# The shift of the exponentials, formed by two subtractions on GpSimd from the fifth pair on, and a new order of all work

## The chip, the cores and the metric

The kernel runs on one core of one Trainium2 chip. Its time is device microseconds of one execution, from the host's side of the launch to the end; a profiled execution also has a span, from the first to the last instruction on the engines. The engines are TensorE (PE in the profile), VectorE (DVE), ScalarE (ACT), GpSimd (POOL) and SyncE (SP, which only issues DMAs here).

## The reference

Eight batches of eight heads of random-feature attention over 576 positions with head size 64 and 128 features, and behind it one dense layer pair (SiLU between) over all 4608 rows, everything in float32:

```python
def phi(x):
    proj = np.einsum('bhsd,md->bhsm', x, omega)
    sq = np.sum(x * x, axis=-1, keepdims=True) / 2.0
    h = proj - sq
    h = h - np.max(h, axis=-1, keepdims=True)
    return np.exp(h) / np.sqrt(m)
kv = np.einsum('bhsm,bhsd->bhmd', k_p, v)
z = np.sum(k_p, axis=2)
num = np.einsum('bhsm,bhmd->bhsd', q_p, kv)
den = np.einsum('bhsm,bhm->bhs', q_p, z)[..., None] + 1e-06
# attention output num / den, as rows of 512 columns, then
h = x @ w_in                                  # 512 -> 2048
g = h * (1.0 / (1.0 + np.exp(-h)))
return g @ w_out                              # 2048 -> 512
```

The exponent of `phi` is `proj - sq - max(proj - sq)`. As `sq` is the same for a whole row, the kernel takes `m`, the largest `proj` of the row, and forms the shift `nb` that is added to `proj` before the exponential from `m` and `s = sq` (kept as `-(m - s) - s`, rounding as the reference rounds).

## The kernel before

**Attention by pairs of heads.** Two heads make a pair: 32 pairs, `n` from 0 to 31. The 2 x 576 positions of a pair lie in nine chunks of 128 rows, four of one head (chunks 0 to 3), four of the other (5 to 8) and a mixed one (4, "the middle"). For keys (`k`) and then queries (`q`) a pair does this:

- ACT squares the rows (L375) and DVE sums the squares to `sq` (L379);
- PE projects the eight side chunks into two PSUM banks (`project`, L402) and the middle into a third (`project_mid`, L409);
- DVE takes the row maxima `mx` (`top`, L418 for the sides, L416 for the middle);
- `shift` forms `nb`, 128 x 8 for the sides and 128 x 1 for the middle, with two instructions each time (L422, L423). For the first `LEAD` = 4 pairs one call covers all nine chunks;
- then either ACT takes nine exponentials straight from PSUM with `nb` as bias (`expo`, L438, for "straight" pairs), or DVE adds `nb` and writes to SBUF (`lower`, L446 and L443) and ACT takes one exponential over all nine chunks later (`expo_all`, L452). Pairs 0 to 7 and the last ones are straight, the bounds being `DIRECT`, `STRAIGHT_K` and `STRAIGHT_Q`.

The banks of the projection are free for the next matmul only when the exponentials or the lowering have read them. Behind the exponentials come the sums of the keys (`sums` on POOL, L459 to L467, or matmuls, L477 and L479, for the first eight pairs), `kv` (L500), the denominators on DVE (`denom`, L488, ten products, and the reciprocal, L493), the scaling of the queries on POOL (`normal`, L518, three instructions), their transposes on PE (`turn`, L524), and the numerators (L562).

**The dense layers.** The first three row tiles go through plain matmuls (`stage1` L737, `stage2` L983), the other six in three groups of two by a Strassen-like scheme of seven block products (`product` L822, `second` L936). Every operand is held as a high and a low part, so that each product takes three matmuls. The weights are rebuilt from 64-bit words by DVE (L660, L662, L666) and split by POOL (L679, L683) in the first 200 us; later POOL forms the sums of weight blocks that the block products need (L715 to L779), and DVE forms the low parts and block sums of the activations (L880, L869, L902, L926).

**What sets the order.** The whole program is a list of units (`Plan.add`) with an engine, an assumed duration, a due time (`key`), what it waits for and which buffers it takes and frees. `Plan.run` goes through them once, when the kernel is built, and picks for each engine the ready unit that is due first; the instructions of every engine are issued in that order and run in it. Constants (`PRO`, `STAY`, `SPREAD_*`, `PREPARE_*`, `PAIRS_*` and so on) set the due times, and `SHIFTS` lists seeds that move some of them at random. Where a bank is free but PE would idle for over 1.0 us in the first 100 us, the plan puts in matmuls of ones (`pulses`, L351) whose result nobody reads.

A unit of the shift is planned like this (sides; the middle alike):

```python
add(("nb", n, who, 0), "DVE", 0.55, at(n, 0, o + 1.4), lambda n=n, who=who: shift(n, who, sides),
    after=[("top", n, who, j) for j in range(2)] + [("ssum",) + w], port=True)
```

Of the kernel before, what the change touches and what calls it, by code (L numbers as in the profile page):

```python
# [14 lines left out]
ALU = mybir.AluOpType  # L15
# [19 lines left out]

LAG = 2
DIRECT = 8
STRAIGHT_K = 22.298
STRAIGHT_Q = 24.404
NARROW = 4  # L40
AHEAD_OUT = 3
LEAD = 4
# [12 lines left out]
for _f in range(16):  # L55
# [15 lines left out]
START_MLP = 57.593  # L71
SLOW = 8.332
MLP_STEP = 2.725
PRO = 18.178
SWITCH = 1.3
STAY = 19.856
HANDOFF = {"PE": 0.25, "ACT": 0.1, "DVE": 0.1, "POOL": 0.15, "SP": 0.2}
CALM = 0.5
SHIFTS = (
# [3 lines left out]
)  # L83
HOT = 100.0
PULSE = 0.24
# [4 lines left out]


STRETCH_0 = 1.362
SLACK = 0.818
PAIRS_4 = 195.050
PAIRS_16 = 39.198
PAIRS_22 = 540.000
PAIRS_28 = -59.566
SPREAD_IN = 2.859
SPREAD_OUT = 10.456
SPREAD_AT = 366.656  # L100
SPREAD_LATE = 469.554
EARLY_SUMS = 18.806
PREPARE_1 = 22.764
PREPARE_2 = 2.035
LEAD_W = 14.593
PREPARE = (PREPARE_1, PREPARE_2)
BEGIN = [clock(NF * PLAIN)]
BEGIN.append(BEGIN[0] + 56 * MLP_STEP * STRETCH_0)
BEGIN.append(BEGIN[1] + 56 * MLP_STEP * SLACK)
RATE = (STRETCH_0, SLACK, SLACK)  # L110
PACE = ((0, clock(0)), (4, PAIRS_4), (16, clock(NF * PLAIN) - PAIRS_16), (22, PAIRS_22), (28, BEGIN[1] - PAIRS_28))

# [52 lines left out]
class Plan:  # L165
# [6 lines left out]
    def add(self, name, eng, dur, key, fn, after=(), order=(), alloc=(), free=(), banks=0, table=None, lat=0.0, port=False, of="att", reads=()):  # L172
        u = dict(
            name=name, eng=eng, dur=dur, key=key, fn=fn, after=list(after), order=list(order), alloc=list(alloc),
            banks=banks, of=of, table=table, lat=lat, port=port or eng == "POOL", reads=list(reads),
        )
        assert name not in self.units, name
        self.units[name] = u
        for i in free:
            self.freed_by.setdefault(i, []).append(name)  # L180

    def run(self, until=None, heat=None):
# [47 lines left out]
        while any(ready.values()):  # L230
            best = None
            for e, us in ready.items():
                pick, least = None, None
                for u in us:
# [26 lines left out]
                    if u["table"] and u["table"] != table:  # L261
                        key += STAY
                    least = t if least is None else min(least, t)
# [53 lines left out]
def attention_mlp(ctx: ExitStack, tc: tile.TileContext, qT, kT, qn, kn, v, om_in, w_in, w_out, out, out_t):  # L317
    nc = tc.nc
# [100 lines left out]

    def shift(n, who, part):  # L420
        m, s, nb = (part(T[a, n, who]) for a in ("mx", "sq", "nb"))
        nc.vector.tensor_tensor(nb, m, s, ALU.subtract)  # L422
        nc.vector.scalar_tensor_tensor(nb, nb, -1.0, s, ALU.mult, ALU.subtract)  # L423

    def every(a):
        return a[:, :NC]
# [569 lines left out]
    add = plan.add  # L996

    def at(n, off, steady):
        if n < LEAD:
            return PRO * n + off  # L1000
        return pace(n - LEAD - 1 + steady / 32)
# [8 lines left out]
    def straight(n, who):  # L1010
        return n < DIRECT or n >= {"k": STRAIGHT_K, "q": STRAIGHT_Q}[who]

# [3 lines left out]
    for n in range(NWIN):  # L1016
        calm = n < LEAD
        for i, who in enumerate("kq"):
# [20 lines left out]
            o = 6.2 + 10.8 * i  # L1039
# [16 lines left out]
            else:  # L1056
                add(md, "PE", 2.2 if whole else 0.25, at(n, 3 * i + 0.1, o + 5.2),
                    lambda ps, n=n, who=who, f=mid_and_squares if whole else project_mid: f(n, who, ps),
# [7 lines left out]
            if calm:  # L1066
                add(("nb", n, who, 0), "DVE", 0.45, at(n, 3 * i + 1.5, 0), lambda n=n, who=who: shift(n, who, every),
                    after=[("top", n, who, j) for j in range(3)] + ([] if whole else [("ssum",) + w]),
                    free=[bk(md)] if whole else [("ss",) + w], port=True)
            else:  # L1070
                add(("nb", n, who, 0), "DVE", 0.55, at(n, 0, o + 1.4), lambda n=n, who=who: shift(n, who, sides),
                    after=[("top", n, who, j) for j in range(2)] + [("ssum",) + w], port=True)
                add(("nb", n, who, 2), "DVE", 0.45, at(n, 0, o + 5.8), lambda n=n, who=who: shift(n, who, middle),
                    after=[("top", n, who, 2), ("ssum",) + w], free=[("ss",) + w], port=True)
            for j in range(3):
                b = bk(md) if j == 2 else bk(pj, j)
                nb = ("nb", n, who, 0 if calm else j & 2)
# [188 lines left out]
    def second_stage(p):  # L1266
        t1 = lambda i, s: last_time(p, TURNS[p].index(i), s)
        last_of = lambda i: TURNS[p][TURNS[p].index(i) - 1]
        for s in range(NS):
            early = product_time(p, s, 6) + 5 if p else last_time(0, 1, s) - EARLY_SUMS  # L1270
            W = lambda i, s=s: ("ws", p, s, i)
# [3 lines left out]
            for what, after, key in (  # L1275
                ("T3", [W(2), W(3)], early), ("T1", [W(0), G("T3")], early + 1), ("T2", [G("T1"), H(0), L(0)], t1(1, s) - (6 if p else EARLY_SUMS)),
                ("T4", [G("T2"), H(2), L(2), W(1)], last_time(p, 5 if p else 3, s) - (12 if p else 0)),
# [80 lines left out]
    for s in range(NS):  # L1358
        before = ("sp", s - 1, len(sums_of) - 1) if s else ("wlo", "out", NF - 1)
        base = clock(NF + 2 + SPREAD_IN * s)  # L1360
        for i, what in enumerate(sums_of):
# [25 lines left out]
    for s in range(NS):  # L1387
        late = s >= NS // 2
        base = (SPREAD_LATE - SPREAD_OUT * (NS // 2) if late else SPREAD_AT) + SPREAD_OUT * s
        before = [("spo", s - 1, len(out_steps) - 1)] if s else []  # L1390
# [199 lines left out]
```

## Time and profile before

| | |
|---|---|
| median of 2 runs | 1021.25 us (1021.1 to 1021.39) |
| the profiled execution's own time | 1022.64 us |
| its span | 1020.8 us |
| mean granted TensorE clock | 0.990 |
| PE busy | 987.1 us, 97% of the span |
| DVE / ACT / POOL busy | 786.1 / 615.5 / 359.3 us |
| DMA | 232.94 MB, mean 228 GB/s |

PE's busy time counts overlapping matmuls as one stretch, and their ends are modelled; so PE's idle time in a stage is what its busy time leaves of it, and a busy PE can still run at a lowered clock, which the profile lists as the granted clock of a stretch (1.00 is full). The rest of a stage's loss is the busy time multiplied by what the clock lacks. By stage, in us: up to 200 the weights are rebuilt beside the first attention pairs; up to 475 the plain tiles run with one pair every 20 us or so between them; up to 730 the block products of the first group run beside the last pairs; after that only block products are left.

### The profile page before, as it was taken

To read this page: it belongs to the slowest core of one execution; us is meant where nothing else is said; L and a number is where in the kernel's file an instruction comes from. 1 tells how busy PE (TensorE), PEld (TensorE's weight loads), DVE (VectorE), ACT (ScalarE), POOL (GpSimd) and SP (SyncE) were. 2 spreads that over 40 slices of the span, in tenths; PEclk is the share of its full clock that TensorE was granted. 3 is DMA by queue.
4 is the path that set the end of the run, shared out by engine and by line. 5 is a ranking of instruction groups with operands and counts; after the bars stand their busy time and mean duration, and the time that the engine had idled before them with its cause. 6 is when DMAs were issued, how large, how long until landed. Compare 5 with 4: busy or idle time off the path is not lost.

```text
span 1020.8 us, 17425 instructions
## 1 busy us (share of the span) xinstructions
PE 987.1 (97%) x5792; PEld 792.2 (78%) x5792; DVE 786.1 (77%) x1895; ACT 615.5 (60%) x1225; POOL 359.3 (35%) x447
## 2 busy tenths in 40 slices
PE   7879998999999999999999998999999999999997
PEld 6757877777777787787777776877878888888886
DVE  5879888877877787888986699998657984556863
ACT  4678676655566666676879685656635553324541
POOL 1425554466757776575563313230100000000000
PEclk9889999999999999999999999999999999999999
DMA  7676667677776777768888665866555568566564
GB/s 286 209 254 202 217 239 255 219 248 243 227 227 211 248 243 236 243 226 300 291 282 295 207 198 179 306 211 235 195 200 202 188 209 258 193 197 195 189 213 154
DMA packets 107592, 232.94 MB, mean 228 GB/s; under 512 B 14704, under 2 KB 39408, under 8 KB 107504
## 3 DMA queue, kind: packets, MB, share of 16 engines
q1 hardware_dynamic: 107200, 231.52, 68.2%
q8 instruction: 46, 0.75, 0.3%
q10 hardware_dynamic: 304, 0.33, 0.1%
q14 instruction: 42, 0.34, 0.1%
HBM read 182.52 MB, written 49.28 MB: 227 GB/s over the span
## 4 chain that ended last, share of the span: by engine, by line
PE 81%; DVE 10%; ACT 4%; DMA 3%; issue 1%; POOL 0%; POOLq 0%; SPq 0%; DVEq 0%; ACTq 0%
PE ps_acc L822 13%; PE ps_acc L936 12%; PE ps_acc L983 11%; PE ps_h L737 11%; PE ps_att L936 4%; PE ps_att L822 3%; PE ps_fx L936 3%; PE ps_att L402 3%; DVE prod L488 2%; PE ps_h L936 2%; PE ps_fx L822 2%; PE ps_fx L402 2%; PE ps_fx L500 2%; PE ps_att L500 1%; PE ps_fx L737 1%
## 5 line engine op out<-in xcount | busy, mean ns | idle before, releaser
L822 PE MATMUL ps_acc<-w,x 128*128 128x512 f32 x696 | 171.9, 396 | 0.9 <-DVE w L869 0.5
L822 PEld LDWEIGHTS ps_acc<-w,x 128*128 128x128 f32 x696 | 127.9, 188 | 29.1 <-DVE w L869 0.7
L518 POOL TENSOR_TENSOR hq<-hq,rd 128x384 f32<-128x384 f32 x96 | 82.2, 882 | 188.6 <-DVE rd L493 152.2
L737 PE MATMUL ps_h<-x,w 128*128 128x512 f32 x504 | 133.9, 403 | 3.3 <-ACT en L536 2.6
L983 PE MATMUL ps_acc<-wo,gh 128*128 128x512 f32 x384 | 124.6, 405 | 0.0
L737 PEld LDWEIGHTS ps_h<-x,w 128*128 128x128 f32 x504 | 92.1, 190 | 24.4 <-ACT en L536 2.8
L936 PE MATMUL ps_acc<-w,x 128*128 128x512 f32 x360 | 94.1, 394 | 0.4 <-DVE w L926 0.4
L983 PEld LDWEIGHTS ps_acc<-wo,gh 128*128 128x128 f32 x384 | 67.9, 188 | 14.5
L936 PEld LDWEIGHTS ps_acc<-w,x 128*128 128x128 f32 x360 | 66.6, 188 | 15.2 <-DVE w L926 0.9
L983 PE MATMUL ps_acc<-wo,gl 128*128 128x512 f32 x192 | 75.2, 392 | 0.0
L488 DVE CUSTOM_DVE_ANT_0 prod<-hq,ps_att 128x128 f32<-128x128 f32 (+1 forms) x160 | 45.9, 287 | 26.3 <-PE ps_att L508 12.0
L936 PE MATMUL ps_acc<-gh,x 128*128 128x512 f32 x160 | 58.2, 393 | 0.0
L375 ACT ACTIVATE nat<-nat 128x576 f32<-128x576 f32 x64 | 44.3, 696 | 20.7 <-DMA nat<-qn 10.8
L880 DVE TENSOR_TENSOR gl<-gf,gh 128x512 fp32r<-128x512 f32 x48 | 39.5, 825 | 13.9 <-ACT gf L876 13.7
L874 ACT ACTIVATE gh<-ps_h 128x512 fp32r<-128x512 f32 x42 | 25.1, 598 | 37.1 <-PE ps_h L737 34.6
L459 POOL TENSOR_TENSOR t<-hk 128x256 f32<-128x256 f32 x48 | 38.3, 817 | 22.6 <-ACT hk L452 20.4
L983 PEld LDWEIGHTS ps_acc<-wo,gl 128*128 128x128 f32 x192 | 36.0, 188 | 8.0
L536 ACT COPY en<-ps_att 128x384 f32<-128x384 f32 x46 | 21.7, 480 | 33.8 <-PE ps_att L524 30.7
L936 PEld LDWEIGHTS ps_acc<-gh,x 128*128 128x128 f32 x160 | 30.1, 188 | 6.3
L822 PE MATMUL ps_att<-w,x 128*128 128x512 f32 x138 | 34.8, 390 | 0.0
L779 POOL TENSOR_TENSOR wraw<-w,wraw 128x256 fp32r<-128x256 f32 x32 | 24.3, 758 | 27.9 <-ACT wraw L777 27.3
L467 POOL TENSOR_TENSOR es<-es,hk 64x128 f32<-64x128 f32 x48 | 26.4, 549 | 19.2 <-ACT hk L438 16.6
(450 smaller groups left out, 2534.7 us busy)
## 6 DMA issues: line engine op xcount, KB each, us to landing
x<-ws SPq DMA_DIRECT2D x84, 512.0 KB, 4.3
x<-wt SPq DMA_DIRECT2D x48, 512.0 KB, 4.0
x<-wo_d SPq DMA_DIRECT2D x72, 256.0 KB, 3.3
wo<-wo_d SPq DMA_DIRECT2D x32, 512.0 KB, 3.9
rawk<-kT SPq DMA_DIRECT2D x32, 352.0 KB, 4.0
rawq<-qT SPq DMA_DIRECT2D x32, 352.0 KB, 4.7
v<-v SPq DMA_DIRECT2D x32, 320.0 KB, 4.5
nat<-kn SPq DMA_DIRECT2D x32, 288.0 KB, 4.2
```

Source lines behind the costliest of these rows:

```text
L375: nc.scalar.activation(nat, nat, AF.Square, scale=SCALE * 0.5**0.5)
L402: nc.tensor.matmul(ps[:, i * M : (i + 1) * M], raw[r, o : o + P], oms[r], start=True, stop=True)
L459: nc.gpsimd.tensor_tensor(T["t", n][:, part], e[:, 5 * part : 5 * part + 2], e[:, 5 * part + 2 : 5 * part + 4], ALU.add)
L467: nc.gpsimd.tensor_tensor(T["es", n][r, j], T["es", n][r, j], e[r, MID], ALU.add)
L488: nc.vector.tensor_tensor_reduce(out=prod[r], in0=e[r, c], in1=z[r, j * M : (j + 1) * M], scale=1.0, scalar=GUARD, op0=ALU.mult, op1=ALU.a ...
L500: nc.tensor.matmul(ps[j * D : (j + 1) * D, :M], vt[:, c + j], e[:, c], start=i == 0, stop=i == 4)
L518: nc.gpsimd.tensor_tensor(e[:, c], e[:, c], rd[:, c].unsqueeze(2).broadcast_to([P, 3, M]), ALU.mult)
L737: nc.tensor.matmul(ph, w[:, i], x[:, j], start=k == 0 and n == 0, stop=k == NK - 1 and n == 2)
L822: nc.tensor.matmul(ph, ws[:, u, kk * P : (kk + 1) * P], o[:, x], start=i in (0, 1, 4) and kk == 0 and n == 0, stop=kk == 1 and n == 2, ski ...
L880: nc.vector.tensor_tensor(gl, T.pop(("gf", t, f)), T["gh", t, f].bitcast(F32), ALU.subtract)
L936: nc.tensor.matmul(T["qb", p, chain][d], w[:, u, d * P : (d + 1) * P], x, start=i in (0, 1, 4) and s == 0 and n == 0, stop=s == NS - 1 and ...
L983: nc.tensor.matmul(T["po", t][j], g[:, js], w, start=f == 0 and n == 0, stop=f == NF - 1 and n == 2)
```

## The change

From pair 4 on, both instructions of `shift` run on GpSimd instead of VectorE: first `nb = s - m`, then `nb = nb - s`, two subtractions of two SBUF operands each (before: `m - s`, and then `-1 * nb - s` in one instruction). The first four pairs keep theirs on VectorE. The units of the shift are on the plan's POOL list, with assumed durations of 0.5 and 0.48 us instead of 0.55 and 0.45. The bounds of the straight pairs fall, so that the keys of pair 22 and the queries of pairs 23 and 24 are now straight as well: nine exponentials each on ACT instead of three additions on DVE and one long exponential. All other constants belong to the plan's due times, and with the new list of seeds the order of all units is another one.

```diff
-STRAIGHT_K = 22.298
-STRAIGHT_Q = 24.404
+STRAIGHT_K = 21.796
+STRAIGHT_Q = 22.472
...
-PRO = 18.178
+PRO = 18.094
 SWITCH = 1.3
-STAY = 19.856
+STAY = 17.152
...
 SHIFTS = (
-    55, 761, 1230, 1684, 2043, 2652, 3396, 5453, 5899, 6430, 7010, 8410, 8796, 9966, 11076, 11672, 12487,
+    41, 994, 1464, 1948, 2437, 3270, 4238, 4360, 4966, 5289, 5786, 6975, 8040, 8520, 8692, 9611, 11187, 11522,
...
-SLACK = 0.818
+SLACK = 0.821
...
-PAIRS_28 = -59.566
-SPREAD_IN = 2.859
-SPREAD_OUT = 10.456
-SPREAD_AT = 366.656
+PAIRS_28 = -42.472
+SPREAD_IN = 2.893
+SPREAD_OUT = 10.080
+SPREAD_AT = 346.870
 SPREAD_LATE = 469.554
-EARLY_SUMS = 18.806
-PREPARE_1 = 22.764
-PREPARE_2 = 2.035
-LEAD_W = 14.593
+EARLY_SUMS = 21.838
+PREPARE_1 = 33.617
+PREPARE_2 = 10.063
+LEAD_W = 13.300
...
     def shift(n, who, part):
         m, s, nb = (part(T[a, n, who]) for a in ("mx", "sq", "nb"))
-        nc.vector.tensor_tensor(nb, m, s, ALU.subtract)
-        nc.vector.scalar_tensor_tensor(nb, nb, -1.0, s, ALU.mult, ALU.subtract)
+        if n < LEAD:
+            nc.vector.tensor_tensor(nb, m, s, ALU.subtract)
+            nc.vector.scalar_tensor_tensor(nb, nb, -1.0, s, ALU.mult, ALU.subtract)
+        else:
+            nc.gpsimd.tensor_tensor(nb, s, m, ALU.subtract)
+            nc.gpsimd.tensor_tensor(nb, nb, s, ALU.subtract)
...
-                add(("nb", n, who, 0), "DVE", 0.55, at(n, 0, o + 1.4), lambda n=n, who=who: shift(n, who, sides),
+                add(("nb", n, who, 0), "POOL", 0.5, at(n, 0, o + 1.4), lambda n=n, who=who: shift(n, who, sides),
...
-                add(("nb", n, who, 2), "DVE", 0.45, at(n, 0, o + 5.8), lambda n=n, who=who: shift(n, who, middle),
+                add(("nb", n, who, 2), "POOL", 0.48, at(n, 0, o + 5.8), lambda n=n, who=who: shift(n, who, middle),
```

Behind `shift`, the lines of the changed kernel have numbers that are higher by four (L518 is L522, L737 is L741). Counted over the whole program, POOL issues 224 instructions more (112 of L426, the first subtraction, and 112 of L427) and DVE 233 fewer: 224 of the shift and nine of the lowering. ACT issues 27 exponentials of one chunk more, three of nine chunks fewer, and two table loads more (72 instead of 70). PE issues seven matmuls of ones more (25 instead of 18) and is otherwise given the same matmuls.

Three places of the new order. The first is **PE where the dense layers begin**, from the middle projection of pair 3's keys on (the pairs are counted from 0). `rawk` and `rawq` are the projections' inputs, `hq` the scaled queries of pair 2 that are transposed, `en` their features for the numerators, `x_` and `w_` the first row tile and the first weight block. Before:

```order
L409 MATMUL ps_fx<-oms,rawk 128x128
L402 MATMUL ps_acc<-oms,rawq 128x128 x8
L524 MATMUL ps_h<-ident,hq 128x128 x9
L409 MATMUL ps_acc<-oms,rawq 128x128
L409 MATMUL ps_acc<-oms,rawk 128x128
L737 MATMUL ps_h<-x_427,w_449 128x512 x3
L737 MATMUL ps_h<-x_646,w_449 128x512 x3
```

Now:

```order
L409 MATMUL ps_acc<-oms,rawk 128x128
L741 MATMUL ps_fx<-x_428,w_460 128x512 x3
L528 MATMUL ps_acc<-ident,hq 128x128 x3
L741 MATMUL ps_fx<-x_644,w_460 128x512 x3
L528 MATMUL ps_h<-ident,hq 128x128 x6
L566 MATMUL ps_h<-en,kw 64x512 x2
L566 MATMUL ps_att<-en,kw 64x64 x2
L402 MATMUL ps_att<-oms,rawq 128x128 x8
L741 MATMUL ps_fx<-x_766,w_460 128x512 x3
```

The nine transposes stood in one run, ahead of the first matmuls of the dense layers; now groups of those stand before, among and behind them, in another bank (`ps_fx`).

The second is **POOL while the weights are split**, from the scaling of one pair's queries on, some 10 us of the stage that ends at 168 us. `w_` and `wo` are the weight blocks (each is split by a CAST and a TENSOR_TENSOR), `hq<-hq,rd` is the scaling, `nbk` and `nbq` are the shifts of keys and queries. Before:

```order
L518 TENSOR_TENSOR hq<-hq,rd 128x384 x2
L679 CAST w_1811<-w_1777 128x512
L683 TENSOR_TENSOR w_1811<-w_1777,w_1811 128x512
L518 TENSOR_TENSOR hq<-hq,rd 128x384
L679 CAST wo<-w_1768 128x512
L683 TENSOR_TENSOR wo<-w_1768,wo 128x512
L679 CAST wo<-w_1804 128x512
L679 CAST w_1930<-w_1901 128x512
```

Now:

```order
L522 TENSOR_TENSOR hq<-hq,rd 128x384 x3
L683 CAST w_1892<-w_1801 128x512
L687 TENSOR_TENSOR w_1892<-w_1801,w_1892 128x512
L426 TENSOR_TENSOR nbk<-sqk,mxk 128x1
L427 TENSOR_TENSOR nbk<-nbk,sqk 128x1
L683 CAST wo<-w_1799 128x512
L687 TENSOR_TENSOR wo<-w_1799,wo 128x512
L683 CAST wo<-w_1830 128x512
L687 TENSOR_TENSOR wo<-w_1830,wo 128x512
L426 TENSOR_TENSOR nbq<-sqq,mxq 128x2x4
L427 TENSOR_TENSOR nbq<-nbq,sqq 128x2x4
```

The shifts stand one by one between the splits of the weights, each time both subtractions together. In the stages behind it the same queue reads `L522 x3`, then shifts of the next pair: of the 112 first subtractions in the program, 46 stand behind an L522 with nothing but other shifts between.

The third is **PE in the middle of the plain tiles**, behind one pair's query projection (L402): from the middle projection of the next pair's keys (one row ahead of it in the first piece) to the second group of transposes. `ps_att` is the bank that the projection and the transposes take in turn. Before:

```order
L737 MATMUL ps_h<-x_1947,w_2218 128x512 x3
L409 MATMUL ps_att<-oms,rawk 128x128
L524 MATMUL ps_att<-ident,hq 128x128 x3
L737 MATMUL ps_h<-x_2282,w_2218 128x512 x3
L524 MATMUL ps_att<-ident,hq 128x128 x3
```

Now:

```order
L409 MATMUL ps_att<-oms,rawk 128x128
L528 MATMUL ps_att<-ident,hq 128x128 x3
L741 MATMUL ps_h<-x_2051,w_2260 128x512 x3
L741 MATMUL ps_h<-x_2330,w_2260 128x512 x3
L987 MATMUL ps_acc<-wo,gh 128x512 x2
L987 MATMUL ps_acc<-wo,gl 128x512
L987 MATMUL ps_acc<-wo,gh 128x512 x2
L987 MATMUL ps_acc<-wo,gl 128x512
L741 MATMUL ps_h<-x_2681,w_460 128x512 x3
L528 MATMUL ps_att<-ident,hq 128x128 x3
```

Three matmuls of the dense layers stood between the first and the second group of transposes; now 15 do.

4 rows, old and new, of the table SHIFTS are left out of this document.

## The prediction

> **What bounds the kernel now.** I read the head of the page first, then the span cut into stages (columns: stretch, its width, busy time and instructions of PE, PE's weight loads, DVE, ACT and POOL, then PE's granted clock, DMA share and GB/s).
>
> ```profile
> span 1020.8 us, 17425 instructions
> PE 987.1 (97%) x5792; PEld 792.2 (78%) x5792; DVE 786.1 (77%) x1895; ACT 615.5 (60%) x1225; POOL 359.3 (35%) x447
> PE 81%; DVE 10%; ACT 4%; DMA 3%; issue 1%; POOL 0%; POOLq 0%; SPq 0%; DVEq 0%; ACTq 0%
> ```
>
> ```profile
> 0.00:48.00 48.00, 39.41 (x334) 33.41 (x336) 34.07 (x108) 29.37 (x86) 14.00 (x23) 0.89 0.72 245
> 48.00:65.00 17.00, 11.73 (x91) 8.66 (x87) 12.54 (x37) 12.37 (x38) 6.64 (x8) 0.80 0.86 282
> 65.00:100.00 35.00, 32.07 (x229) 25.20 (x228) 31.99 (x89) 26.53 (x64) 15.46 (x16) 1.00 0.62 204
> 150.00:168.00 18.00, 14.26 (x94) 11.72 (x95) 15.15 (x27) 15.08 (x28) 7.99 (x9) 0.91 0.83 273
> 168.00:200.00 32.00, 30.72 (x179) 24.22 (x178) 27.73 (x65) 18.00 (x28) 15.56 (x16) 1.00 0.61 213
> 200.00:475.00 275.00, 274.79 (x1776) 217.48 (x1774) 218.77 (x610) 172.62 (x303) 184.57 (x235) 1.00 0.73 238
> 475.00:600.00 125.00, 122.84 (x795) 96.12 (x795) 99.32 (x289) 100.22 (x209) 57.87 (x84) 1.00 0.78 265
> 600.00:625.00 25.00, 21.72 (x138) 16.89 (x137) 23.74 (x58) 14.12 (x39) 6.83 (x6) 1.00 0.49 160
> 730.00:1000.00 270.00, 269.89 (x1198) 222.40 (x1197) 180.27 (x292) 120.38 (x206) 2.40 (x3) 1.00 0.63 207
> 1000.00:1020.80 20.80, 14.94 (x65) 11.73 (x63) 5.35 (x8) 2.22 (x4) 0.00 (x0) 0.98 0.40 123
> ```
>
> PE is the bound, and the change leaves its matmuls as they are. So nothing can be won but what PE loses: idle time, which is width less busy time, and busy time multiplied by what the clock lacks. That gives 8.6 + 4.3 = 12.9 us up to 48; 5.3 + 2.3 = 7.6 up to 65; 2.9 up to 100; 3.7 + 1.3 = 5.0 in 150 to 168 and 1.3 up to 200; 0.2 in the 275 us behind that; 2.2 in 475 to 600; 3.3 in 600 to 625; 5.9 + 0.3 = 6.2 in the tail. The first 48 us hold the pairs whose shift stays on VectorE, and the tail holds no shift and reads the same in the new order, so both are left alone. What can move is 7.6 + 2.9 + 6.3 + 2.2 + 3.3 = **22.3 us**. DVE's share of 77%, and its 10% of the chain, are not a prize in themselves.
>
> Next I looked at what PE waited for in those stages. These are PE's rows of the timeline; in brackets stand the idle time ahead and what ended it.
>
> ```profile
> 52.13 0.52 PE L524 MATMUL ps_h<-ident,hq 128*128 128x128 f32 x3 [0.66 <-ACT en L536]
> 53.31 0.52 PE L524 MATMUL ps_h<-ident,hq 128*128 128x128 f32 x3 [0.66 <-ACT en L536]
> 58.39 2.93 PE L737 MATMUL ps_h<-x,w 128*128 128x512 f32 x6 [2.62 <-ACT en L536]
> 163.56 0.79 PE L477 MATMUL ps_fx<-hk,sides 128*128 128x128 f32 x2 [2.55 <-ACT hq L438]
> 614.18 0.34 PE L402 MATMUL ps_h<-oms,rawq 64*128 64x128 f32 x1 [1.11 <-DVE den L488]
> 619.03 0.50 PE L936 MATMUL ps_acc<-gl,x 128*128 128x512 f32 x1 [1.19 <-DVE gl L926]
> ```
>
> **The change, part by part.** First what DVE is rid of. Two answers group the shift's lines from 60 us on, and two give the durations (least, median, most) of its keys' half.
>
> ```profile
> 60.00:1020.80 960.80, 35.26 (x110) 1.00 0.68 226
> 60.00:1020.80 960.80, 38.42 (x110) 1.00 0.68 226
> L422 DVE TENSOR_TENSOR nbk<-mxk,sqk x60: 144/169/808, 11.3 to 720.6; 128x8 f32<-128x8 f32 x28, 128x1 f32<-128x1 f32 x28, 128x9 f32<-128x9 f32 x4
> L423 DVE SCALAR_TENSOR_TENSOR nbk<-nbk,sqk x60: 158/169/754, 11.5 to 720.8; 128x8 f32<-128x8 f32 x28, 128x1 f32<-128x1 f32 x28, 128x9 f32<-128x9 f32 x4
> ```
>
> So 220 of the 224 instructions take 35.3 + 38.4 = 73.7 us, where 110 x (0.144 + 0.158) = 33 us is what they take undisturbed. The other 40 us are something else, and the place of the 2.55 us wait shows what:
>
> ```profile
> 158.07 1.28 POOL L683 TENSOR_TENSOR w<-w,w 128x512 fp32r<-128x512 f32 x1
> 159.31 1.28 POOL L683 TENSOR_TENSOR wo<-w,wo 128x512 fp32r<-128x512 f32 x1
> 159.40 1.20 DVE L423 SCALAR_TENSOR_TENSOR nbq<-nbq,sqq 128x1 f32<-128x1 f32 x1
> 161.84 1.28 ACT L438 ACT_TABLE_LOAD   x1
> 163.14 0.37 ACT L438 ACTIVATE hq<-ps_fx,nbq 128x128 f32<-128x128 f32 x1
> ```
>
> One column should take DVE 0.16 us; it took 1.20, from 159.40 to 160.60, and ended with POOL's instruction (159.31 + 1.28 = 160.59). A small DVE instruction with two SBUF operands stands still while POOL works on two of its own. The Trainium skill ("SBUF — State Buffer", section "SBUF: two separate sides") calls the port that the two engines share an exclusive lock; these rows agree.
>
> On POOL, the change adds 224 instructions of a size that before doesn't show. The nearest are these:
>
> ```profile
> L467 POOL TENSOR_TENSOR es<-es,hk x48: 447/456/973, 207.8 to 722.0; 64x128 f32<-64x128 f32 x48
> L766 POOL TENSOR_TENSOR w<-w,w x24: 724/734/1065, 211.7 to 384.0; 128x256 f32<-128x256 f32 x24
> L683 POOL TENSOR_TENSOR w<-w,w x16: 1262/1296/1622, 27.1 to 196.0; 128x512 fp32r<-128x512 f32 x16
> ```
>
> From 256 to 512 columns the least rises by 538 ns, 2.1 ns a column; 724 less 256 of these leaves 186 ns for none, and 128 columns (447) lie on the same line. I take 0.20 us for 8 columns and 0.19 for one. The ends are DVE's own 0.144 (32 us for 224) and 0.447 (100 us); at 0.2 it is 45 us, 359 to 404 us of POOL. In 200 to 475, its fullest stage, POOL is 67% busy, and all 45 us there would make it 84%, so as load this costs nothing. The price, if any, is in the queue: a shift now stands behind what POOL was given before it.
>
> The lowering and exponentials:
>
> ```profile
> L446 DVE TENSOR_TENSOR hq<-ps_att,nbq 128x512 f32<-128x512 f32 x20 | 13.4, 683 | 0.6
> L443 DVE TENSOR_SCALAR hk<-ps_att,nbk 128x128 f32<-128x128 f32 x15 | 5.3, 351 | 0.6
> L438 ACT ACTIVATE hk<-ps_att,nbk 128x128 f32<-128x128 f32 x86 | 24.5, 385 | 6.3 <-DVE nbk L423 6.2
> L452 ACT ACTIVATE hq<-hq 128x1152 f32<-128x1152 f32 x17 | 19.7, 1160 | 0.9 <-DVE hq L443 0.9
> ```
>
> DVE loses 6 x 0.683 + 3 x 0.351 = 5.2 us. ACT gains 27 x 0.385 - 3 x 1.16 + two table loads of 1.28 (row of 161.84) = 9.5 us. Before, ACT's fullest of the late stages is 475 to 600 (100.2 of 125), so 25 us of slack hide it. If that cover is gone, a bank comes free by 4 x 0.385 - 0.683 = 0.86 us later at six banks, 5 us. DVE is rid of 79 us in all.
>
> Now stage by stage, on PE's path.
>
> *48 to 65.* The three waits for `en` L536 add up to 3.94 us. They come from nine transposes in one run in one bank, with the first dense matmuls behind them in that bank. In the new order three dense matmuls stand before and between the groups, in `ps_fx`. A matmul takes 269.89 / 1198 = 0.225 us, so each three cover 0.68, as long as the short waits, and the bank of the long one is another. I take **-3.5**; the ends are -7.6 (clock too) and +3.8, one stall like that at 163.56 with its clock loss (2.55 + 1.28).
>
> *65 to 100.* DVE is 91% busy and PE loses 2.9. Four subtractions a pair go; I take **-1** (-2.9 to +3.8).
>
> *150 to 200.* The shift ahead of 163.14 took 0.92 + 1.20 us on DVE by the same waiting; on POOL it is 0.4 behind at most one split (1.28). The table load stays. I take **-2**, of 6.3 (-6.3 to +2.6, the rest of a split and a table load once more).
>
> *475 to 625.* Of 5.4 us lost, the waits at 614 and 619 are for DVE, which is 95% full there; but few of the shifts lie in those 25 us. I take **-2** (-5.4 to +3).
>
> *Fresh waits.* In 200 to 475 PE loses next to nothing, so any new order can only lose there. I take **+2.5**, two thirds of a stall of 3.8 (0 to +8, two of them).
>
> Sum: -3.5 - 1 - 2 - 2 + 2.5 = **-6**. The profiled execution took 1022.64 us, 1.84 beyond its span and 1.39 above the median of 1021.25; so it would take 1016.6, and the median **1015**.
>
> **Rivals.** *A, the wait only moves.* POOL gets 224 more instructions on two SBUF operands, and what is left on DVE with two such operands waits for them as the shift did. The 40 us of DVE waiting then return on other lines, and the gains that rest on DVE (-1, -2, -2) go; the first place's -3.5 stays against 2.5 of fresh waits: 1020, say 1018 to 1024. For it: the 1.20 us row. Against: a new instruction holds POOL for 0.2 us, no more than 45 in all, and most DVE lines read PSUM. The Trainium skill ("Perfetto Trace Analysis", section "Optimizing Scalar/DVE Operations") says that offloading between these two engines might not help since they share a port; no row of before shows it for this load.
>
> *B, slower: POOL's queue ties the shift to the pair before.* One pair in the middle:
>
> ```profile
> 315.54 0.22 DVE L493 RECIPROCAL rd<-den 128x9 f32<-128x9 f32 x1
> 315.83 2.41 POOL L518 TENSOR_TENSOR hq<-hq,rd 128x384 f32<-128x384 f32 x3 [0.38 <-DVE rd L493]
> 317.51 0.76 DVE L423 SCALAR_TENSOR_TENSOR nbq<-nbq,sqq 128x8 f32<-128x8 f32 x1
> ```
>
> The shift ended at 318.27, and the scaling at 318.24. In the new order the shifts of the next keys' middle and queries' sides stand behind the scaling, which waits for `rd`: four subtractions, 0.8 us, and a handover of 0.1 as between DVE and POOL here, so 319.15, 0.9 us later. Over 22 such pairs that is 20 us if every late bank stops PE: 1035 with my other terms, 1041 with no gain elsewhere, 1025 if half of them do. It decides where PE needs the bank within 0.9 us. Three matmuls between the transposes, as before, would cover 0.7; the 15 of the new order cover 3.4, which speaks against it.
>
> *C, nearly all that can move goes.* Less nine tenths of 22.3: 1001 (999 to 1004). Against it stand the table loads and five separate causes.
>
> That the shift isn't moved is excluded by the order: 112 and 112 on POOL.
>
> **How the numbers follow.** Forecast 0.62 (own range 1007 to 1022, from the ends above, few of which can fall together), A 0.18, B 0.12, C 0.08. A range of 1004 to 1030 holds the forecast's cases and A, with half of B and a little of C. Two per cent, about what a measurement of this kernel can tell from no change, is 20.4 us: faster is below 1000.8, half of C and the forecast's far end, 0.05; slower is above 1041.7, B's far end and several stalls together, 0.05; within, 0.90.
>
> **What would show it.** Right: DVE's busy time near 707 us (786 less 79), POOL's near 404, subtractions of 0.2 us; the three waits for L536 around 52 to 58 gone; PE's loss outside start and tail near 16. For A: DVE above 735, its other lines longer. For B: in 200 to 475, PE waits for L438 or L446 with a late L427 ahead of them. Wrong altogether: a changed time with the same PE loss, that is, other matmul times or another clock.

## The result, and the profile after

The changed kernel takes 1031.34 us (median of 1030.91 and 1031.76), against 1021.25 before: a ratio of **1.0098**, 95% interval 1.0079 to 1.0117. It is slower by 10 us where 6 us less were forecast, and the time lies outside the range of 1004 to 1030. The profiled execution took 1031.76 us.

The head of its page, with the shares of the chain below:

```profile
span 1030.0 us, 17421 instructions
PE 992.0 (96%) x5806; PEld 798.3 (78%) x5806; DVE 722.2 (70%) x1662; ACT 623.2 (61%) x1251; POOL 423.4 (41%) x671
PE 88%; DVE 6%; ACT 3%; issue 1%; POOL 1%; DMA 1%; DVEq 0%; POOLq 0%; ACTq 0%
```

VectorE has lost 64 us of busy time and GpSimd has gained 64. The relief is there, and the kernel is slower all the same. So the span was cut into stages again, with a cut at 460 and 490 (columns as in the prediction). After:

```profile
48.00:65.00 17.00, 12.51 (x84) 8.83 (x82) 14.62 (x35) 11.31 (x33) 7.09 (x10) 0.80 0.83 264
65.00:100.00 35.00, 31.26 (x209) 24.77 (x208) 28.12 (x79) 26.94 (x66) 19.49 (x28) 0.90 0.68 226
150.00:200.00 50.00, 47.42 (x288) 38.46 (x288) 40.19 (x78) 31.56 (x59) 31.33 (x40) 0.97 0.64 209
200.00:460.00 260.00, 260.00 (x1660) 206.13 (x1657) 161.02 (x450) 161.24 (x285) 189.31 (x311) 1.00 0.75 242
460.00:490.00 30.00, 18.75 (x113) 14.16 (x112) 21.97 (x58) 14.93 (x29) 23.26 (x38) 0.83 0.61 207
490.00:600.00 110.00, 109.64 (x760) 86.93 (x760) 70.30 (x214) 95.92 (x210) 51.95 (x108) 1.00 0.75 248
600.00:625.00 25.00, 23.46 (x139) 18.17 (x137) 24.76 (x41) 20.93 (x47) 8.82 (x16) 1.00 0.60 194
```

The kernel before, where this cut differs from the one shown:

```profile
150.00:200.00 50.00, 44.98 (x272) 35.94 (x273) 42.88 (x91) 33.08 (x56) 23.55 (x24) 0.97 0.69 235
460.00:490.00 30.00, 29.41 (x193) 22.91 (x192) 26.15 (x68) 22.21 (x41) 15.28 (x19) 1.00 0.84 299
490.00:600.00 110.00, 108.43 (x699) 85.07 (x699) 87.13 (x255) 87.27 (x186) 51.18 (x73) 1.00 0.76 257
```

PE's loss (idle time, and busy time multiplied by what the clock lacks) by stage, after against before: 48 to 65, 7.0 against 7.6; 65 to 100, 6.9 against 2.9; 150 to 200, 4.0 against 6.4; 490 to 625, 1.9 against 4.9; and **460 to 490, 11.3 + 3.2 = 14.4 against 0.6**. That one place costs 13.8 us, more than the whole difference; 65 to 100 takes 4 more, and 150 to 200 and 490 to 625 give back 5.3.

What PE waits for there, in the timeline (in brackets the idle time ahead):

```profile
466.22 0.52 PE L528 MATMUL ps_att<-ident,hq 128*128 128x128 f32 x3 [1.59 <-DVE hk L447]
469.45 0.37 PE L402 MATMUL ps_att<-oms,rawk 64*128 64x128 f32 x1 [1.31 <-ACT en L540]
474.20 2.40 PE L504 MATMUL ps_fx<-hk,v 128*64 128x128 f32 x20 [3.35 <-DVE hk L450]
476.35 1.39 PE L566 MATMUL ps_att<-en,kw 128*64 128x512 f32 x4
483.27 0.46 PE L409 MATMUL ps_att<-oms,rawk 128*128 128x128 f32 x2 [3.29 <-DVE den L492]
484.89 2.74 PE L826 MATMUL ps_acc<-w,x 128*128 128x512 f32 x6
```

These are the steps of one pair and the next, each waiting for the step before it on ACT, DVE and POOL, with nothing between them. The last plain matmul (L987) starts at 464.2. The block products (L826), but for one group at 455, begin at 484.89; their operands are built from the numerators of pairs 12 to 19, and pair 19's are the row at 476.35. The kernel before at the same place:

```profile
461.08 1.14 PE L562 MATMUL ps_att<-en,kw 128*64 128x512 f32 x8
463.65 1.52 PE L822 MATMUL ps_h<-w,x 128*128 128x512 f32 x6
```

There, pair 19's numerators come at 461.08, 15 us sooner, and block products stand beside plain ones from 463.65 on. The order of PE tells why. These are the dense matmuls (plain and block products) that PE is given from the middle projection of one pair's queries (L409) to that of the next pair, counted from the two orders:

```
pair (to the next)   9  10  11  12  13  14  15  16  17  18 | 9 to 19 | 19  20  21
before              57  60  51  63  51  54  60  63  75  63 |   597   | 69  81  48
after               66  63  60  66  60  66  63  63  75  87 |   669   | 57  12  84
```

From pair 9 to 19 the new order spends 72 dense matmuls more; at the 0.225 us of the prediction that is 16 us. In the traces the middle projection of pair 9's queries is 1.1 us later than before (221.27 and 220.18), that of pair 19's 15.8 us (444.77 and 429.01). The 72 are missing from pair 20 to 21: 12 instead of 81. No PE time goes at 250 to 460; it goes when the plain work has run out.

### The profile page after: what moved, and what is told of

The parts are those of the page before. It is cut to its first block, busy times and chain, and to the rows that moved or that the text cites. A ratio compares the mean times of both kernels' runs of the same rounds, so it can differ in the third digit from the quotient of the medians.

```text
span 1030.0 us, 17421 instructions
## 1 busy us (share of the span) xinstructions
PE 992.0 (96%) x5806; PEld 798.3 (78%) x5806; DVE 722.2 (70%) x1662; ACT 623.2 (61%) x1251; POOL 423.4 (41%) x671
## 4 chain that ended last, share of the span: by engine, by line
PE 88%; DVE 6%; ACT 3%; issue 1%; POOL 1%; DMA 1%; DVEq 0%; POOLq 0%; ACTq 0%
PE ps_acc L826 16%; PE ps_acc L940 15%; PE ps_acc L987 13%; PE ps_h L741 11%; PE ps_att L402 3%; PE ps_h L940 3%; PE ps_fx L940 3%; PE ps_att L826 3%; PE ps_att L940 2%; DVE prod L492 2%; PE ps_fx L741 2%; PE ps_fx L826 2%; PE ps_att L566 2%; PE ps_att L504 2%; PE ps_h L826 1%; PE ps_fx L402 1%
## 5 line engine op out<-in xcount | busy, mean ns | idle before, releaser
L826 PE MATMUL ps_acc<-w,x 128*128 128x512 f32 x738 | 184.4, 397 | 0.0
L826 PEld LDWEIGHTS ps_acc<-w,x 128*128 128x128 f32 x738 | 136.4, 189 | 29.4
L522 POOL TENSOR_TENSOR hq<-hq,rd 128x384 f32<-128x384 f32 x96 | 87.5, 936 | 117.0 <-DVE rd L497 114.9
L741 PE MATMUL ps_h<-x,w 128*128 128x512 f32 x492 | 130.2, 401 | 0.0
L987 PE MATMUL ps_acc<-wo,gh 128*128 128x512 f32 x384 | 122.3, 399 | 0.0
L940 PE MATMUL ps_acc<-w,x 128*128 128x512 f32 x402 | 107.0, 392 | 0.0
L741 PEld LDWEIGHTS ps_h<-x,w 128*128 128x128 f32 x492 | 88.6, 188 | 20.0 <-ACT gf L880 0.9
L940 PEld LDWEIGHTS ps_acc<-w,x 128*128 128x128 f32 x402 | 74.8, 188 | 15.9
L987 PEld LDWEIGHTS ps_acc<-wo,gh 128*128 128x128 f32 x384 | 69.5, 188 | 14.5
L492 DVE CUSTOM_DVE_ANT_0 prod<-hq,ps_att 128x128 f32<-128x128 f32 (+1 forms) x200 | 57.4, 287 | 30.8 <-ACT kw L517 9.5
L987 PE MATMUL ps_acc<-wo,gl 128*128 128x512 f32 x192 | 75.2, 392 | 2.6 <-DVE gl L884 2.6
L940 PE MATMUL ps_acc<-gh,x 128*128 128x512 f32 x180 | 67.3, 395 | 1.4 <-DMA x<-wt 1.4
L426 POOL TENSOR_TENSOR nbq<-sqq,mxq 128x8 f32<-128x8 f32 (+1 forms) x56 | 22.8, 407 | 69.1 <-DVE mxq L418 34.9
L884 DVE TENSOR_TENSOR gl<-gf,gh 128x512 fp32r<-128x512 f32 x48 | 44.3, 923 | 9.0 <-ACT gf L880 9.0
L987 PEld LDWEIGHTS ps_acc<-wo,gl 128*128 128x128 f32 x192 | 36.0, 188 | 10.9 <-DVE gl L884 3.0
L426 POOL TENSOR_TENSOR nbk<-sqk,mxk 128x8 f32<-128x8 f32 (+1 forms) x56 | 16.0, 286 | 49.7 <-DVE mxk L416 33.7
L418 DVE TENSOR_REDUCE mxq<-ps_att 128x4 f32<-128x512 f32 x37 | 24.1, 676 | 17.2 <-PE ps_fx L402 8.6
L402 PE MATMUL ps_att<-oms,rawk 64*128 64x128 f32 x288 | 34.5, 286 | 1.5 <-ACT en L540 1.3
```

Of the source, the lines that this page charges most:

```text
L402: nc.tensor.matmul(ps[:, i * M : (i + 1) * M], raw[r, o : o + P], oms[r], start=True, stop=True)
L426: nc.gpsimd.tensor_tensor(nb, s, m, ALU.subtract)
L492: nc.vector.tensor_tensor_reduce(out=prod[r], in0=e[r, c], in1=z[r, j * M : (j + 1) * M], scale=1.0, scalar=GUARD, op0=ALU.mult, op1=ALU.a ...
L522: nc.gpsimd.tensor_tensor(e[:, c], e[:, c], rd[:, c].unsqueeze(2).broadcast_to([P, 3, M]), ALU.mult)
L741: nc.tensor.matmul(ph, w[:, i], x[:, j], start=k == 0 and n == 0, stop=k == NK - 1 and n == 2)
L826: nc.tensor.matmul(ph, ws[:, u, kk * P : (kk + 1) * P], o[:, x], start=i in (0, 1, 4) and kk == 0 and n == 0, stop=kk == 1 and n == 2, ski ...
```

## The experiments

Two theories stood at the start. **Order**: the loss comes of where the new order leaves PE without dense work. **Queue**: it comes of the shift on GpSimd, behind the scalings and splits (the prediction's rival B). All ratios are to the kernel before, run on the same chip.

**Engine and order apart.** The first two runs keep the order of all instructions word for word and change only the engine on which the shift is issued.

x1, against the changed kernel:

```diff
-        if n < LEAD:
-            nc.vector.tensor_tensor(nb, m, s, ALU.subtract)
-            nc.vector.scalar_tensor_tensor(nb, nb, -1.0, s, ALU.mult, ALU.subtract)
-        else:
-            nc.gpsimd.tensor_tensor(nb, s, m, ALU.subtract)
-            nc.gpsimd.tensor_tensor(nb, nb, s, ALU.subtract)
+        nc.vector.tensor_tensor(nb, m, s, ALU.subtract)
+        nc.vector.scalar_tensor_tensor(nb, nb, -1.0, s, ALU.mult, ALU.subtract)
```

x2, against the kernel before (its units stay on the plan's VectorE list):

```diff
-        nc.vector.tensor_tensor(nb, m, s, ALU.subtract)
-        nc.vector.scalar_tensor_tensor(nb, nb, -1.0, s, ALU.mult, ALU.subtract)
+        if n < LEAD:
+            nc.vector.tensor_tensor(nb, m, s, ALU.subtract)
+            nc.vector.scalar_tensor_tensor(nb, nb, -1.0, s, ALU.mult, ALU.subtract)
+        else:
+            nc.gpsimd.tensor_tensor(nb, s, m, ALU.subtract)
+            nc.gpsimd.tensor_tensor(nb, nb, s, ALU.subtract)
```

> The changed kernel's order of all work, every instruction at the same place, but both instructions of the shift issued on VectorE as before. Theory 'order': what cost the 10 us is the place at 460 to 490 us where PE has no dense work left beside a pair; that place is in the order, so the time stays at 1029 to 1036, with 10 us or more of PE's loss still in 460 to 490, and DVE busy again by about 60 us more. Theory 'queue': the subtractions behind the scalings on GpSimd's queue cost it; then the time falls to 1019 to 1024 and the loss in 460 to 490 shrinks to under 4 us.

> The kernel before with its own order, every instruction at the same place, but the shift of pairs 4 to 31 issued as two subtractions on GpSimd. Theory 'order': the engine alone costs nothing or saves a little, 1014 to 1022, DVE busy down by about 70 us. Theory 'queue': subtractions now stand behind scalings and weight splits that the order did not reckon with, and PE stops for them in many pairs: 1028 or more.

Measured: the new order with the shift on VectorE takes 1053.41 us, ratio 1.0314 (1.0298 to 1.0329). The old order with the shift on GpSimd takes 1020.75, ratio **0.9986** (0.9975 to 0.9996). So the engine's part is a gain of 1.4 us in the old order and of 22 us in the new one, and the order's part is a loss of 11 us with the shift on GpSimd and of 32 with it on VectorE. Theory 'queue' falls for x2 outright. Of x1, 'order' had only the sign: it expected 1029 to 1036. Stages of x1:

```profile
460.00:490.00 30.00, 23.32 (x153) 17.51 (x153) 20.97 (x54) 18.38 (x35) 16.13 (x20) 0.83 0.72 244
490.00:600.00 110.00, 102.31 (x678) 80.15 (x675) 82.09 (x255) 85.40 (x189) 49.64 (x68) 0.97 0.68 225
```

The hole is still there (6.7 + 4.0 us), and as much again follows in 490 to 600, most of it up to 510. The shift also comes later in x1: from the end of a row maximum to the end of its shift the traces give 2.07 us in the mean (from 60 us on), against 1.30 in the changed kernel. In the old order it is 1.10 on VectorE (before) and 1.06 on GpSimd (x2). So the new order, laid out for GpSimd, pays when the shift comes later; that all 22 us come of this isn't shown. In x2 the place is whole, and DVE is relieved as much as in the changed kernel:

```profile
PE 986.6 (97%) x5792; PEld 791.0 (78%) x5792; DVE 722.5 (71%) x1671; ACT 615.8 (60%) x1225; POOL 416.4 (41%) x671
460.00:490.00 30.00, 29.44 (x193) 23.23 (x193) 23.35 (x58) 22.62 (x40) 17.22 (x28) 1.00 0.84 301
163.25 0.49 PE L481 MATMUL ps_fx<-hk,sides 128*128 128x128 f32 x2 [1.24 <-ACT hq L442]
```

The 2.55 us wait of before at 163.56 is 1.24 here. The table load between the shift and that exponential stays, as forecast.

**Which part of the new order: numbers or units?** x3 plans and issues the shift on GpSimd with all numbers of the kernel before; x4 plans and issues it on VectorE with the new numbers.

> The changed kernel's units (shift planned and issued on GpSimd) with all constants and seeds of the kernel before: the order is computed anew from the old numbers. Theory 'order': the time depends on where this order happens to leave PE uncovered, so anywhere in 1016 to 1036, and its difference from 1021 is found as loss at one or two places. Theory 'queue': 1028 or more, spread over many pairs of 200 to 730.

> The changed kernel's constants and seeds, but the shift planned and issued on VectorE as before: again another order. Theory 'order': 1016 to 1036 by what this order leaves uncovered, not by the engine. Theory 'queue': no subtraction on GpSimd, so 1017 to 1025 with no loss of over 4 us at any place between 200 and 730.

1055.56 us, ratio 1.0332 (1.0314 to 1.0349), and 1047.12 us, ratio 1.0248 (1.0221 to 1.0275). Both lie above the 1036 that 'order' gave as its upper end, and by 'queue' x4 should have been near 1021. An order computed anew from numbers chosen for another list of units is 25 to 34 us slower, on either engine. The new numbers win 24 us of that back (x3 against the changed kernel) but not the last 10.

The two orders lose in different ways. x3, like the changed kernel, has 8 of the 384 plain units (three matmuls each) left when it comes to pair 20's query projection, and most of its loss stands in one place. x4 has 39 left there, where the kernel before has 42, and loses in several. The place in x3, and two of those in x4 below it:

```profile
460.00:540.00 80.00, 61.85 (x416) 46.47 (x415) 58.68 (x160) 50.88 (x97) 56.42 (x96) 0.87 0.72 246
```

```profile
480.00:500.00 20.00, 15.44 (x89) 11.54 (x87) 16.32 (x49) 12.59 (x26) 10.27 (x14) 0.83 0.67 226
600.00:650.00 50.00, 44.44 (x239) 35.12 (x238) 46.10 (x109) 34.34 (x73) 14.17 (x16) 0.93 0.51 162
```

26 us in x3, and 7.2 and 8.7 us in x4. So an order that keeps its plain work can be slow as well.

**Does using up the plain work make the hole?** d1 and d2 take x2 (old order, shift on GpSimd), use its places as due times, and hold each pair's query projection from pair 10 on behind more of the plain units. Without the last line of the edit below, these due times give the order of x2 again, unit for unit; so what differs from x2 is the doing of that line.

```diff
+    dense = [u for u in seen if u["name"][0] in ("s1", "s2")]
+    ...
+        if 10 <= n <= 20:          # at the query projection u of pair n
+            u["order"].append(dense[past + int(3.1 * (n - 9)) - 1]["name"])   # d2: 1.55
```

> The old order with the shift on GpSimd, and one rule more: from pair 10 on each pair may only start its query projection behind three more units of the plain dense work (nine matmuls) per pair than before, so that by pair 20 only 8 of the 384 plain units are left, as in the changed kernel (there 8, in the order before 42). Nothing else is changed. Theory 'cover' (the hole at 460 to 490 us is there because plain work is used up before pairs 19 and 20 are through): PE loses 9 to 15 us more in 450 to 500 and the time is 1029 to 1036. Theory 'scattered' (the changed order is slower by many small waits, the hole would be made up elsewhere): 1020 to 1025.

> As the run before, with half the rule: 22 plain units are left at pair 20 and 8 at pair 21. Theory 'cover': a hole about half as large or less, 1021 to 1029, later in time than in the run before. Theory 'scattered': the same time as without the rule, 1020 to 1023.

d1: 1046.09 us, ratio 1.025 (1.0228 to 1.0271). d2: 1039.08, ratio 1.0186 (1.0161 to 1.0212). The stage of d1, and of x2 below it:

```profile
460.00:500.00 40.00, 24.17 (x132) 18.67 (x131) 26.17 (x75) 19.18 (x36) 27.83 (x43) 0.70 0.56 187
```

```profile
460.00:500.00 40.00, 38.98 (x260) 30.81 (x260) 30.98 (x82) 31.53 (x58) 23.76 (x42) 1.00 0.81 285
```

d1 loses 15.8 + 7.3 = 23 us where x2 loses 1, of the 27 us by which it is slower. So the hole can be made in a good order by this one rule, which 'scattered' excludes; it is larger than the 9 to 15 us expected. d2 fits less well: 1039 where 1021 to 1029 was expected. It loses 6.9 us in 460 to 490, 9.7 in 500 to 550 and 6.6 in 600 to 650 (x2: 0.6, 0.2 and 3.2). The second may be the later hole of which 'cover' spoke; the third is none, so a rule that changes the order costs beyond the place it aims at.

**Another order with cover.** y1 takes the places of the old order as due times and plans the shift on GpSimd's list.

```diff
+        if u["name"][0] == "nb" and u["name"][1] >= LEAD:
+            u["eng"], u["dur"] = "POOL", 0.48
```

> The places of the old order taken as due times, and the shift planned on GpSimd's list from pair 4 on: another order of all work again, in which plain work lasts through pairs 20 and 21 (78 and 57 dense matmuls between the query projections there, 57 and 12 in the changed kernel). Theory 'cover': no loss of over 4 us between 440 and 520, and 1014 to 1026. Theory 'an order planned with the shift on GpSimd is slow': 1028 or more, as in the changed kernel and with the old numbers.

1039.97 us, ratio 1.0181 (1.0157 to 1.0206): a miss for 'cover'. The plain work lasts through pairs 20 and 21, and still 5.5 us go at 480 to 490, with 3.5 at 80 to 90, 4 at 540 and 3.5 at 620. The hole is one way in which an order loses, not the only one.

**GpSimd from pair 8 on.** y2 is x2 with `n < DIRECT` in place of `n < LEAD`.

> The old order, with the shift on GpSimd from pair 8 on only, so that pairs 4 to 7, which run while GpSimd splits the weights, keep it on VectorE. If splits hold the subtractions up there, 1018 to 1020; if it is the waiting of VectorE for the splits that matters (the 2.55 us wait of the kernel before at 163.56), 1021 to 1023.

1020.55 us, ratio 0.9989 (0.9980 to 0.9999). It can't be told from x2: with their intervals of about 1 us, the four pairs beside the weight splits are worth no more than that either way.

**What lateness costs, and where.** z1 (old order) and z2 (new order) issue the first subtraction three times.

```diff
             nc.gpsimd.tensor_tensor(nb, s, m, ALU.subtract)
+            nc.gpsimd.tensor_tensor(nb, s, m, ALU.subtract)
+            nc.gpsimd.tensor_tensor(nb, s, m, ALU.subtract)
```

> The old order with the shift on GpSimd, the first subtraction issued three times instead of once (the result is the same), so that every shift comes 0.4 us later and holds GpSimd 0.4 us longer: 224 more instructions of 0.2 us. Theory 'cover': the lateness falls on waits that PE has work beside, 1020 to 1024. Theory 'queue' (my slower rival, by which 0.9 us of lateness in each of 22 pairs stops PE): two shifts of a pair behind one scaling, 0.8 us a pair, 17 us, 1035 to 1040.

> The changed kernel with the first subtraction issued three times. Where plain work stands beside a pair nothing is lost; in 460 to 490 us, where none does, each of about three shifts on the chain of a pair costs 0.4 us or a little more. Theory 'cover': 1032 to 1036. Theory 'queue': 1045 or more.

z1: 1041.18 us, ratio 1.0198 (1.0177 to 1.0219), 22 us above x2. z2: 1041.58, ratio 1.0203 (1.0180 to 1.0227), 11 us above the changed kernel, between the two theories. 'Cover' is refuted in z1: PE does not have enough work beside each pair to hide 0.4 us a shift. That left open whether the lateness did it or GpSimd's occupation. z3 issues the same two subtractions behind the shift, into a spare tile:

> The old order with the shift on GpSimd, and behind each shift two more subtractions of the same size into a spare tile that nobody reads: GpSimd is as busy as with the triple subtraction, but the shift isn't later. Theory 'lateness': 1020 to 1027. Theory 'occupation' (GpSimd's time and the port it shares with VectorE): 1035 to 1043, as with the triple subtraction.

1024.45 us, ratio 1.003 (1.0020 to 1.0041), 4.5 us above x2. GpSimd is as busy in both, z1 first:

```profile
PE 994.9 (96%) x5792; PEld 797.3 (77%) x5792; DVE 719.0 (69%) x1671; ACT 615.8 (59%) x1225; POOL 470.4 (45%) x895
```

```profile
PE 987.4 (97%) x5792; PEld 790.6 (77%) x5792; DVE 725.2 (71%) x1671; ACT 616.5 (60%) x1225; POOL 465.1 (45%) x895
```

So some four fifths of z1's cost is lateness on the chain of a pair: the shift ends 0.66 us later than in x2 in the mean, in z3 only 0.10 later (measured from the row maximum, as above). z6 makes the shift late on VectorE, in the kernel before, in the same way (from pair 4 on):

> The kernel before, shift on VectorE, with the first subtraction issued three times from pair 4 on: every shift comes 0.3 us later where VectorE is undisturbed, more where GpSimd works, and VectorE has 224 instructions more. Theory 'lateness': 1035 to 1050, as for the triple subtraction on GpSimd or more. Theory 'occupation of GpSimd': 1022 to 1030.

1065.44 us, ratio 1.0413 (1.0375 to 1.0450), beyond its upper end. VectorE's busy time rises by 60 us (845.9 after 786.1), 0.53 us a shift, and 42 us of it reach the end. On GpSimd the triple subtraction added 54 us of busy time (470.4 after 416.4 in x2), 0.48 us a shift, and 22 us of it reached the end. So of the time added to the shift 40 to 70% was paid. Lateness alone doesn't explain z6's higher price: its shift ends 0.70 us later than before in the mean, hardly more than z1's 0.66. VectorE is also occupied for longer, and no run put the spare subtractions behind the shift there to price that. The other way, one subtraction in place of two (zero less the maximum; the half square is neither subtracted nor added back, which changes the rounding only):

```diff
-            nc.gpsimd.tensor_tensor(nb, s, m, ALU.subtract)
-            nc.gpsimd.tensor_tensor(nb, nb, s, ALU.subtract)
+            nc.gpsimd.tensor_tensor(nb, part(zero), m, ALU.subtract)
```

> The old order with the shift on GpSimd formed by one subtraction, zero less the maximum: the half of the square is neither subtracted nor added back, which changes the rounding only. Every shift comes 0.2 us or a little more earlier, 112 instructions less. Theory 'lateness': half of the slope of the triple subtraction, 10 us, if it holds downwards; since PE loses only 16 us outside start and tail, 1011 to 1018. Theory 'nothing left to win': the old order waits for other things, 1019 to 1021.

> The changed kernel with the shift formed by one subtraction, zero less the maximum (rounding only). Theory 'lateness': 4 to 8 us less, 1023 to 1027, by shorter waits in 460 to 490 and elsewhere. Theory 'cover': the hole needs dense work, not a faster shift: 1028 to 1031, 12 us or more still lost in 460 to 490.

In the old order 1017.66 us, ratio 0.9964 (0.9948 to 0.9980), about 2 us below x2 (the two intervals just overlap) and the fastest kernel of this study, at the weak end of what 'lateness' expected. In the new order 1032.01, ratio 1.0103 (1.0084 to 1.0122): nothing is won, as 'cover' expected to within a microsecond. Its hole:

```profile
460.00:490.00 30.00, 21.48 (x111) 15.75 (x109) 22.23 (x53) 15.12 (x28) 20.77 (x31) 0.72 0.63 214
```

8.5 + 6.0 = 14.5 us: the idle part shrinks from 11.3, the clock's part grows from 3.2. An earlier shift does not mend the hole.

**Can the hole be mended by keeping plain work back?** r2 and r3 take the changed kernel's places as due times and hold two or three more plain units per pair back until the pair's query projection is issued.

```diff
+        if 10 <= n <= 20:
+            for d in dense[past - min(2 * (n - 9), 2 * 10) : past]:   # r3: 3 in place of 2
+                d["order"].append(u["name"])
```

> The changed kernel's places taken as due times, with one rule: from pair 10 on, two plain units more per pair are kept back until the pair's query projection is issued, so that 28 of 384 are left at pair 20 instead of 8. Theory 'cover': pairs 10 to 19 go through earlier, the hole at 460 to 490 shrinks by 5 us or more, 1020 to 1028. If the chain of a pair (maxima, shift, lowering, exponential, sums, denominators, scaling) is itself what takes the 21 us of a step, PE waits in 230 to 450 instead, and the time is 1031 or more.

> As the run before with three units per pair, 38 left at pair 20. Theory 'cover': 1016 to 1026. If the chain of a pair is what takes the step, PE waits in 230 to 450 more than in the run before, and the time is 1036 or more.

1111.64 us, ratio 1.0875 (1.0843 to 1.0906), and 1135.15, ratio 1.1116 (1.1092 to 1.1140). 'Cover' is refuted as a recipe. In r2 PE waits where there was nothing to wait for; r2, and before below it:

```profile
230.00:450.00 220.00, 188.88 (x1090) 148.89 (x1087) 106.25 (x308) 113.16 (x199) 143.40 (x240) 0.90 0.61 202
```

```profile
230.00:450.00 220.00, 219.79 (x1438) 173.68 (x1437) 172.03 (x503) 135.75 (x244) 148.07 (x193) 1.00 0.73 234
```

Pair 19's numerators come later, not sooner (554.70 instead of 476.35): with the plain work held back, the chain of the pair sets the pace. The rule also moves work on the other engines, so it isn't shown that no order with the new numbers' chain could be quicker. From pair 9's numerators to pair 19's a step takes 21.2 us in x2, 22.4 in the changed kernel and 30.2 in r2.

## Why the prediction was wrong

*Right.* The bound: PE's loss is the account, and DVE's busy time is no prize. 64 us less of it were worth 1.4 us in x2. The price of a subtraction on GpSimd, forecast at 0.19 to 0.20 us, by the changed kernel (least, median, most):

```profile
L426 POOL TENSOR_TENSOR nbk<-sqk,mxk x56: 189/205/638, 58.5 to 725.9; 128x8 f32<-128x8 f32 x28, 128x1 f32<-128x1 f32 x28
L427 POOL TENSOR_TENSOR nbk<-nbk,sqk x56: 189/204/721, 58.8 to 726.5; 128x8 f32<-128x8 f32 x28, 128x1 f32<-128x1 f32 x28
```

In the mean it was more: 58.5 us for 220 of them in x2, 0.27 each, so that GpSimd came to 416 us there and to 423 in the changed kernel, not 404; what held the longer ones wasn't worked out.

*150 to 200* gave -2.4, where -2 was forecast. *475 to 625*, also forecast at -2, went from 5.4 to 9.6, as the end of the hole lies in it; behind the hole, 490 to 625 gave -3. In x2, where the engine alone differs, 150 to 200 gave -1.5 and 490 to 625 gave -1.1. So the wait at 163.56 was read rightly, but part of both gains is the new order's, and that the first number came out so close is in part luck.

*Rival A* held for a quarter of the waiting. DVE should have come to 707 us; it is 722. In x2, with the same lowering as before, 63.6 us of the shift's 73.7 are gone, so about 10 us of the 40 us of waiting moved to other instructions of VectorE. No stage of x2 loses as much as 1 us more than before. The Trainium skill ("Perfetto Trace Analysis", "Optimizing Scalar/DVE Operations") says that offloading between these two engines might not help; here it helped by 1.4 us in one order and 22 in another.

*48 to 65* was forecast at -3.5 and gave -0.6. The three waits for L536 are down to two, but others stand in their place:

```profile
51.19 0.55 PE L528 MATMUL ps_acc<-ident,hq 128*128 128x128 f32 x3 [0.73 <-POOL hq L522]
53.41 0.52 PE L528 MATMUL ps_h<-ident,hq 128*128 128x128 f32 x3 [0.66 <-ACT en L540]
54.50 1.08 PE L566 MATMUL ps_h<-en,kw 128*64 128x512 f32 x4 [0.57 <-ACT en L540]
56.57 0.48 PE L402 MATMUL ps_att<-oms,rawq 64*128 64x128 f32 x2 [0.69 <-ACT hk L442]
58.76 0.59 PE L402 MATMUL ps_att<-oms,rawq 64*128 64x128 f32 x2 [1.71 <-ACT xr L595]
```

4.4 us in all, against 3.9. I had counted what three dense matmuls cover at each old wait, and not what the rows behind them wait for.

*65 to 100* was forecast at -1 and gave +3.9. Two pairs' denominators stand one behind the other on DVE (72.0 to 79.4), PE waits 1.60 and 0.89 us for the scalings behind them (77.00 and 80.37), and the granted clock of 80 to 90 falls to 0.77.

*The step that failed* is the term for fresh waits: +2.5, with +8 as its end, where one place took 13.8. It was sized by the largest single stall of before, at 163.56. The new stall was of another kind, a whole pair without dense work; and the order, which I had, shows it. I counted cover at one place (15 matmuls in place of 3) and took it as a gain, where the new order was spending early what pair 20 would need. Counting on to the end of the plain work gives 12 dense matmuls where 81 stood. A step of a pair takes some 20 us, and 12 matmuls fill 2.7. Of the 14.4 us lost there 11.3 are waiting and 3.2 the lowered clock that came with it (0.83).

*Rival B* gave the right direction through the wrong place. Its price was of the right size: 0.9 us of lateness in each of 22 pairs was to cost up to 20 us, and z1's shifts, four to a pair and 0.66 us later in the mean, cost 22. But on GpSimd the shift was no later than before (1.06 us behind the row maximum in x2, 1.10 before), since on VectorE it had waited for GpSimd in any case: x2 is 1.4 us faster, not slower. The "cover of 3.4 us" that I held against B belongs to the new order. There z2's shifts came 0.81 us later and cost 11 us, half of what z1 cost in the old order; whether that cover made the difference wasn't tried.

*What stays open.* Which of the numbers spends the plain work early wasn't tried one by one. Nor is it shown that the new order had a choice: r2 and r3 held the work back and were slower, so its chains may need the longer steps. d1 shows that using up the plain work makes such a hole, not that the changed kernel could do without. Every order computed anew (x3, x4, y1) was 18 to 34 us slower than the old one, so changing one number alone would measure that scatter.

## What to carry to other kernels

When a change both moves an operation and recomputes a static order, price them apart: the old order with the new engine, and the new order with the old engine, are two kernels, and here the two parts have opposite signs. In an order in which one dense stream covers the latency of many chains, count how much of that stream is left at each step until it ends; a place with more cover than before may only be spending what a later one needs. (It is one check and not the only one: x4 and y1 kept their dense work and were slow.) An instruction of 0.2 us on the chain of every step can be worth more than tens of microseconds of busy time of its engine.

## What the runs showed of the hardware

Two subtractions of 8 columns or one, put ahead of a result that others wait for, cost five times as much as two of the same size behind it (22 and 4.5 us for 224 of them), on the same engine. What was left on VectorE beside a busier GpSimd grew little: of 40 us of waiting, about 10 came back on its other lines in x2.
